# Sink tokens of a windowed attention in tiled matmuls: four column tiles for their scores, two row tiles for their AV, and a new order of the AV work

## The chip, the cores and the metric

The kernel runs on one core of a Trainium2 chip. A core has TensorE (PE: matmuls; its weight loads are listed apart as PEld), VectorE (DVE), ScalarE (ACT), GpSimd (POOL, which here also issues the input DMAs) and SyncE (SP, which issues DMAs). Matmuls write to PSUM, which the kernel uses as eight banks of 128 x 512 float32; VectorE and ScalarE read the results from there. The metric is the time of one execution in microseconds (us) on the device. Profiles come from one execution each, and their times are counted from the start of its span.

## The reference

Attention in which each query sees the first 4 keys (the sink) and the last 128, then a gated feed-forward network:

```python
batch, n_heads, seq, head_dim = (4, 8, 768, 64)      # n_sink 4, window 128
scores = scale * np.matmul(q, k.transpose(0, 1, 3, 2))
rel = pos[:, None] - pos[None, :]
keep = (pos[None, :] < n_sink) | ((rel >= 0) & (rel < window))
a = softmax(np.where(keep, scores, -1e9))             # over the keys
x = np.matmul(a, v)                                   # as (3072 tokens, 512)
xn = x / np.sqrt(np.mean(x * x, axis=-1, keepdims=True) + 1e-06) * rms_g
g = xn @ w_gate                                       # 512 -> 1536
out = (g * (1.0 / (1.0 + np.exp(-g))) * (xn @ w_val)) @ w_out
```

All inputs and the output are float32; the kernel works in bfloat16 with float32 sums.

## The kernel before

**Blocks and groups.** The 4 x 768 tokens are 24 blocks of 128 tokens: block g is tile t = g % 6 of batch b = g // 6. Four blocks make a group for the feed-forward network (FFN), so there are six groups.

**Attention of a block.** Queries and keys are transposed to `qkT` (features on partitions; two heads share 128 partitions) either on TensorE with a copy by ScalarE (`unit_t`, `unit_t1`) or, for later blocks, by DMA transposes that SP issues. `unit_s(g)` makes the scores of key block g against query blocks g and g + 1 in four PSUM banks (`pT`): eight matmuls over 64 partitions, two heads at a time in the upper and lower half of the array. ScalarE takes the exponential into `et`, and VectorE (batches 0 and 1) or GpSimd (2 and 3) masks it. `unit_av(g, u)` makes the attention output of four heads (half u) of query block g in one bank (`pv`): per head one matmul with the masked scores of key block g − 1 and one with those of block g, 65 columns each, of which the last is the sum of the weights. VectorE divides (`rden`, `x`), ScalarE squares and sums (`sq`, then a read of its accumulator), and after both halves VectorE makes the RMS factor (`m`, `y`) and the normalised rows `xr`. These are transposed to `xnt` on TensorE with a copy by ScalarE (`unit_x`, blocks 0 to 7) or by DMA through SP (from block 8).

**Sink keys.** Blocks with t of 0 and 1 have the sink inside their window; the other 16 blocks get it apart. `unit_sink(b)`, once per batch, makes two tiles. `ksk` holds the four sink keys of each pair of heads; its slices are placed so that a full 128-column weight puts head pair hp at 8 rows of the result from hp x 8 on. `vsk` holds the sink values of all heads on the rows of their own head, zero elsewhere: a matmul with `sel` repeats the values of the four sink tokens for every head (`pvs`), and VectorE multiplies by the mask `headm`. `unit_sink_scores(b, t)`, for t of 2 and 4, adds four full matmuls of 256 columns into one bank (`pss`, L321), which gives the sink scores of two query blocks, and ScalarE takes the exponential (`esk`). `unit_av` starts each half with one full 260-column matmul of `esk` with `vsk` (L444).

**FFN of a group.** For each of twelve feature tiles a gate part (`pg`: four matmuls, then tanh to `th` on ScalarE) and a value part (`pvl`: four matmuls, then two VectorE operations, `p` from `th` and `pg`, and `hT` from `p` and `pvl`). Then for each block of the group three output parts of four matmuls into one bank (`po`), a copy to `osb` by ScalarE and a DMA to the result. A part of the first group is smaller where a pair of feature tiles covers half the tokens.

**Order.** The order of PE and SP is written by hand; that of ScalarE, VectorE and GpSimd is made by a scheduler when the kernel is built and is then fixed. `step(g)` lists the attention work of one step in four slots, and `weave` lays the slots among the FFN parts, one about every 2.25 parts. In step g slot 0 holds the scores of block g (then, for some blocks, `unit_x(g - 3)`), slot 1 the first AV half of block g − 1 (and the sink units), slot 3 the second half, slot 1 or 2 the transposes of a later block. Before these steps stand a prologue and a first group whose order is written out. All PSUM tiles with tag `b1` come in turn from the same eight banks, so each new tile waits until the one eight tiles earlier has been read.

**GpSimd's queue.** It issues the loads of q, k, v and of the weights in a written order, with the selections that make `ident`, `amasks`, `sel` and `headm` among them.

Of the kernel before, what the change touches and what calls it, by code (L numbers as in the profile page):

```python
# [9 lines left out]
ALU = mybir.AluOpType  # L10
ACT = mybir.ActivationFunctionType
FP32 = mybir.dt.float32
BF16 = mybir.dt.bfloat16
I32 = mybir.dt.int32

P = 128
# [12 lines left out]
def kernel(  # L29
# [13 lines left out]
    nc = tc.nc  # L43

    B, H, S, D = q.shape
    DM = H * D
    DFF = moe_w_gate.shape[1]
    NS = int(n_sink)
    assert int(window) == P and NS == 4
    assert D == 64 and H == 8 and S % P == 0  # L50
    NT = S // P
# [4 lines left out]
    GB = 4  # L56
# [1 line left out]
    GN = GB * P  # L58
    VW = D + 1
    HW = 4 * VW  # L60
    KSW = P + 2 * NS
    inv_sqrt_d = 1.0 / math.sqrt(D)
    NEG = -32768.0
    RMS_EPS = 1e-6 * RSQRT_SCALE ** 2
# [86 lines left out]
    nc.vector.memset(amasks[:, 1, 0, :], 0.0)  # L151
    masks = const.tile([P, 2, 2, P], BF16, name="masks")

    sel = const.tile([P, P], BF16, name="sel")
    nc.vector.memset(sel, 0.0)
    headm = const.tile([P, H], BF16, name="headm")
    nc.vector.memset(headm, 1.0)

# [23 lines left out]
    with tc.manual_schedule(engines={mybir.EngineType.Pool, mybir.EngineType.DVE}):  # L184
        load_q(1)
        nc.gpsimd.affine_select(
            out=ident, in_=ident, compare_op=ALU.not_equal, fill=1.0,
            base=0, pattern=[[-1, P]], channel_multiplier=1,
        )
        nc.gpsimd.affine_select(  # L190
            out=amasks[:, 1, 0, :], in_=amasks[:, 1, 0, :], compare_op=ALU.is_ge,
            fill=NEG, base=0, pattern=[[1, P]], channel_multiplier=-1,
        )
        nc.vector.tensor_scalar(
            out=amasks[:, 1, 1, :], in0=amasks[:, 1, 0, :], scalar1=-1.0, scalar2=NEG,
            op0=ALU.mult, op1=ALU.add,
        )
        nc.vector.tensor_copy(out=amasks[:, 0, :, :], in_=amasks[:, 1, :, :])
        nc.vector.memset(amasks[0:NS, 0, :, :], 0.0)
        unit_cast(0)  # L200
        unit_cast(1)
        load_k(1)
        load_v(0)
        load_v(1)
        load_w(0)
        load_q(2)
        load_k(2)
        load_w(1)
        load_q(3)
        load_v(2)  # L210
        load_k(3)
        load_v(3)
        nc.gpsimd.affine_select(
            out=sel[:, 0:H * NS].rearrange("p (h s) -> p h s", s=NS),
            in_=sel[:, 0:H * NS].rearrange("p (h s) -> p h s", s=NS),
            compare_op=ALU.not_equal, fill=1.0,
            base=0, pattern=[[0, H], [-1, NS]], channel_multiplier=1,
        )
        nc.gpsimd.affine_select(
            out=headm, in_=headm, compare_op=ALU.is_ge, fill=0.0,  # L220
            base=0, pattern=[[-NS, H]], channel_multiplier=1,
        )
        nc.gpsimd.affine_select(
            out=headm, in_=headm, compare_op=ALU.is_ge, fill=0.0,
            base=NS - 1, pattern=[[NS, H]], channel_multiplier=-1,
        )
        load_w(2)
        load_w(3)
        load_q(4)
        load_w(4)  # L230
        load_k(4)
        load_w(5)
        load_v(4)
        for g in range(GB + 1, 2 * GB):
            load_q(g)
            load_k(g)
            load_v(g)
        load_wo(0)
        last_load = load_wo(1)
# [51 lines left out]
    def unit_sink(b):  # L291
        ks = sink.tile([P, HP * KSW], BF16, name="ksk")
        nc.vector.memset(ks, 0.0)
        ksv = ks.rearrange("p (h c) -> p h c", c=KSW)
        for hi in range(2):
            pr = slice(hi * D, (hi + 1) * D)
            nc.vector.tensor_copy(
                out=ksv[pr, :, hi * NS:(hi + 1) * NS],
                in_=QKT[b][pr, 1, :, 0:NS],
            )  # L300
        KSK[b] = ks
        vs = sink.tile([P, H, VW], BF16, name="vsk")
        for half in range(2):
            ps = pp[0].tile([P, 512], FP32, name="pvs", tag="b1")
            hs = slice(half * 4, half * 4 + 4)
            nc.tensor.matmul(
                out=ps[:, 0:HW], lhsT=sel, rhs=V16[b][:, 0, hs, :],
                start=True, stop=True,
            )
            nc.vector.tensor_tensor(  # L310
                out=vs[:, hs, :], in0=ps[:, 0:HW].rearrange("p (h c) -> p h c", c=VW),
                in1=headm[:, hs].unsqueeze(2).to_broadcast((P, 4, VW)), op=ALU.mult,
            )
        VSK[b] = vs

    def unit_sink_scores(b, t):

        w = 2 * P
        ps = pp[0].tile([P, 512], FP32, name="pss", tag="b1")
        for hp in range(HP):  # L320
            nc.tensor.matmul(  # L321
                out=ps[:, 0:w], lhsT=KSK[b][:, hp * P:(hp + 1) * P],
                rhs=QKT[b][:, 0, hp, t * P:(t + 2) * P],
                start=(hp == 0), stop=(hp == HP - 1),
            )
        es = sink.tile([P, w], BF16, name="esk", bufs=3)
        nc.scalar.activation(out=es, in_=ps[:, 0:w], func=ACT.Exp, scale=inv_sqrt_d)
        ESK[(b, t)] = es[:, 0:P]
        ESK[(b, t + 1)] = es[:, P:w]
# [105 lines left out]
    def halves(g):  # L435

        return [slice(0, DM // 2), slice(DM // 2, DM)] if g == 1 else [slice(0, DM)]

    def unit_av(g, u):
        b, t = divmod(g, NT)  # L440

        pv = pp[0].tile([P, 512], FP32, name="pv", tag="b1")
        if t >= 2:
            nc.tensor.matmul(  # L444
                out=pv[:, 0:HW], lhsT=ESK[(b, t)],
                rhs=VSK[b][:, 4 * u:4 * u + 4, :],
                start=True, stop=False, skip_group_check=True,
            )
        for i, h in enumerate(range(H)[heads_of(g, u)]):
            dest = pv[:, i * VW:(i + 1) * VW]  # L450
            if t >= 1:
# [184 lines left out]
    def step(g):  # L636
# [2 lines left out]
        b, t = divmod(g, NT)  # L639
        slots = [[], [], [], []]  # L640
        if g < NB:
            slots[0].append(lambda: unit_s(g))
            if t == 1:
                slots[1].append(lambda: unit_sink(b))
            if t in (2, 4):
                slots[1].append(lambda: unit_sink_scores(b, t))
        if g <= NB:
            slots[1].append(lambda: unit_av(g - 1, 0))
            slots[3].append(lambda: unit_av(g - 1, 1))
        if g - 3 < NB:  # L650
            slots[0].append(lambda: unit_x(g - 3))
        if g + 2 < NB and not by_dma(g + 2):
            slots[2 if t != 5 else 1].append(lambda: unit_t(g + 2))
        if g + 3 < NB and by_dma(g + 3):
# [59 lines left out]
    with tc.manual_schedule(engines=MANUAL):  # L714
# [6 lines left out]
        for ft in range(FA, FTN):  # L721
# [2 lines left out]
            [lambda: unit_t1(2, 1), lambda: unit_bias(1, 1), lambda: unit_sp(1, 1), lambda: unit_sink(0)],  # L724
            [lambda: unit_t1(3, 0), lambda: unit_s(2)],
            [lambda: unit_sink_scores(0, 2)],
            [lambda: unit_t1(3, 1), lambda: unit_bias(3, 0), lambda: unit_av(2, 0), lambda: unit_sp(3, 0), lambda: unit_av(2, 1)],
            [lambda: unit_av(3, 0)],
            [lambda: unit_av(3, 1), lambda: unit_t1(4, 0)],
            [lambda: unit_bias(3, 1), lambda: unit_sp(3, 1)],  # L730
            [lambda: unit_x(2)],
            [lambda: unit_t1(4, 1)],
            [lambda: unit_x(3)],
        ], first=True)
        slots = [[lambda: unit_t1(5, 0)], [lambda: unit_t1(5, 1)], [lambda: unit_s(4)], [lambda: unit_sink_scores(0, 4)], [lambda: unit_t(6)], []]
        for g in range(5, NB + 3):
            slots += step(g)
        slots[6].pop()
        slots[10].pop()
        outs = []  # L740
        n = 0
        for G in range(NG):
# [47 lines left out]
```

The softmax here doesn't subtract the row's maximum and nothing guards it: scores larger than these inputs give would overflow.

## Time and profile before

| | us |
|---|---|
| median of 4 runs (lowest to highest) | 254.87 (253.96 to 255.2) |
| the profiled execution's own time | 253.96 |
| its span, from the first to the last instruction | 252.2 |
| PE busy | 240.5 |
| VectorE busy | 180.5 |
| ScalarE busy | 139.4 |
| GpSimd busy | 97.8 |

The rows of the instructions that the diff touches (line, engine, operation, output from inputs, shapes, count, total busy us and mean ns of one; the array's rows and columns stand before the operand of a matmul):

```profile
L456 PE MATMUL pv<-v,et 128*128 128x65 bf16 x168 | 15.3, 193 | 0.0
L444 PE MATMUL pv<-vsk,esk 128*128 128x260 bf16 x32 | 8.8, 274 | 0.1
L321 PE MATMUL pss<-qkT,ksk 128*128 128x256 bf16 x32 | 4.8, 273 | 0.0
L327 ACT ACTIVATE esk<-pss 128x256 bf16<-128x256 f32 x8 | 3.3, 413 | 0.0
L310 DVE TENSOR_TENSOR vsk<-pvs,headm 128x260 bf16<-128x260 f32 x8 | 3.2, 419 | 0.0
L306 PE MATMUL pvs<-v,sel 128*128 128x260 bf16 x8 | 1.6, 277 | 0.0
L293 DVE MEMSET ksk<- 128x272 uint32 x4 | 1.1, 285 | 0.0
L219 POOL TENSOR_SCALAR_AFFINE_SELECT headm<-headm 128x8 bf16<-128x8 bf16 x1 | 0.3, 287 | 0.0
```

A matmul's duration runs to the modelled end of its pipeline, and the next one starts long before that, so the time that a matmul takes from PE is read from one start to the next and not from these means. In the answers in order of time the first number of a row is the start and the second the length in us; rows of equal instructions are merged (x8), and a bracket tells how long the engine was idle before and what ended it. A few matmul records are missing from the trace.

### The profile page before, as it was taken

The numbers are of one execution on the slowest core, as the hardware profiler recorded it, in microseconds if no ns is written. First come the engines' busy times: TensorE is split into PE (matmuls) and PEld (weight loads), VectorE is DVE, ScalarE is ACT, GpSimd is POOL, SyncE is SP. The second block draws the span as 40 slices with busy tenths as digits, with TensorE's granted clock in tenths as the row PEclk, the third lists the DMA queues.
The fourth block names the chain that finished last, engine by engine and source line by source line (L and its number), as shares of the span: only waits on it lengthen the run. The fifth ranks groups of instructions, "written<-read, shape, count | busy, mean of one in ns | idle before, by whom it ended". The sixth has DMA issues, their size and how long they took to land.

```text
span 252.2 us, 4804 instructions
## 1 busy us (share of the span) xinstructions
PE 240.5 (95%) x1733; PEld 128.5 (51%) x1760; DVE 180.5 (72%) x474; ACT 139.4 (55%) x312; POOL 97.8 (39%) x129
## 2 busy tenths in 40 slices
PE   6988989989999999999999999999999999999994
PEld 2537778755555454454454454454454544444441
DVE  5475898899778999439988459988359991287700
ACT  2567668789886465556474546466545341323211
POOL 8996778289986663134041004044301000000000
PEclk9999999999999999999999999999999999999999
DMA  9999999999999999950130550330321013200022
GB/s 130 151 173 192 187 157 189 184 155 150 194 185 166 150 129 154 165 141 8 21 60 6 146 146 3 64 61 17 112 84 23 0 21 100 89 0 0 0 86 83
DMA packets 105849, 25.74 MB, mean 102 GB/s; under 512 B 95073, under 2 KB 102753, under 8 KB 105826
## 3 DMA queue, kind: packets, MB, share of 16 engines
q0 software_dynamic: 80704, 13.90, 76.0%
q1 hardware_dynamic: 24082, 11.28, 19.0%
q10 hardware_dynamic: 1040, 0.26, 0.5%
q8 instruction: 14, 0.23, 0.4%
q14 instruction: 9, 0.07, 0.1%
HBM read 28.31 MB, written 6.29 MB: 137 GB/s over the span
## 4 chain that ended last, share of the span: by engine, by line
PE 72%; DMA 12%; POOL 7%; DVE 5%; issue 2%; ACT 1%; POOLq 0%; ACTq 0%; DVEq 0%
PE po L622 24%; PE pvl L581 19%; PE pg L581 19%; DMA ks<-in_k_dram 5%; DMA wv<-in_moe_w_val_dram 4%; DMA wg<-in_moe_w_gate_dram 3%; PE pT L413 3%; POOL v L124 2%; POOL qs L111 2%; PE pv L456 2%; PE pv L452 1%; PE pv L444 1%; DVE p L599 1%; POOL ks L111 1%; DVE hT L607 1%
## 5 line engine op out<-in xcount | busy, mean ns | idle before, releaser
L581 PE MATMUL pg<-xnt,wg 128*128 128x512 bf16 (+1 forms) x317 | 73.5, 352 | 1.4 <-ACT xnt L567 0.7
L581 PE MATMUL pvl<-xnt,wv 128*128 128x512 bf16 (+1 forms) x322 | 73.4, 353 | 0.3
L622 PE MATMUL po<-wo,hT 128*128 128x512 bf16 x279 | 64.9, 379 | 0.5 <-issue 0.2
L594 ACT ACTIVATE th<-pg 128x512 bf16<-128x512 f32 x72 | 42.9, 596 | 38.6 <-PE pg L581 38.5
L599 DVE SCALAR_TENSOR_TENSOR p<-th,pg 128x512 bf16<-128x512 bf16 x72 | 49.0, 680 | 20.2 <-ACT th L594 19.8
L607 DVE TENSOR_TENSOR hT<-p,pvl 128x512 bf16<-128x512 bf16 x72 | 49.3, 685 | 3.7 <-PE pg L581 0.5
L581 PEld LDWEIGHTS <-wg 128*128 128x128 bf16 x328 | 30.4, 98 | 27.3 <-issue 1.3
L581 PEld LDWEIGHTS <-wv 128*128 128x128 bf16 x328 | 30.5, 98 | 27.1 <-issue 1.1
L422 ACT ACTIVATE et<-pT 128x512 bf16<-128x512 f32 x76 | 39.8, 602 | 4.9 <-PE pT L413 4.7
L622 PEld LDWEIGHTS <-hT 128*128 128x128 bf16 x288 | 26.7, 98 | 29.7 <-issue 0.8
L390 POOL TENSOR_SCALAR_AFFINE_SELECT et<-et 128x512 bf16<-128x512 bf16 x20 | 13.1, 658 | 74.0 <-ACT et L422 74.0
L494 ACT ACTIVATE sq<-x 128x256 bf16<-128x256 bf16 x48 | 20.0, 417 | 26.5 <-DVE x L484 26.1
L629 ACT ACTIVATE osb<-po 128x512 f32<-128x512 f32 x24 | 14.4, 602 | 25.8 <-PE po L622 20.8
L111 POOL DMA_DIRECT2D qs<-in_q_dram x23 | 20.7, 898 | 9.1 <-DMA wo<-in_moe_w_out_dram 2.2
L111 POOL DMA_DIRECT2D ks<-in_k_dram x23 | 20.5, 893 | 5.7 <-DMA wo<-in_moe_w_out_dram 2.9
L124 POOL DMA_DIRECT2D v<-in_v_dram x24 | 21.4, 893 | 3.1 <-DMA wg<-in_moe_w_gate_dram 1.4
L484 DVE TENSOR_TENSOR x<-pv,rden 128x256 bf16<-128x256 f32 x48 | 20.2, 422 | 0.8
L541 DVE SCALAR_TENSOR_TENSOR xr<-x,y,gb 128x512 bf16<-128x512 bf16 (+1 forms) x25 | 19.9, 798 | 0.7
L479 DVE RECIPROCAL rden<-pv 128x4 f32<-128x4 f32 x48 | 8.4, 176 | 16.1 <-PE pv L456 15.9
L388 DVE TENSOR_TENSOR et<-et,masks 128x1024 bf16<-128x1024 bf16 (+1 forms) x22 | 13.9, 638 | 2.8 <-ACT et L422 2.7
L456 PE MATMUL pv<-v,et 128*128 128x65 bf16 x168 | 15.3, 193 | 0.0
L452 PE MATMUL pv<-v,et 128*128 128x65 bf16 x136 | 12.7, 193 | 0.0
(75 smaller groups left out, 216.1 us busy)
## 6 DMA issues: line engine op xcount, KB each, us to landing
out_dram<-osb SPq DMA_DIRECT2D x24, 256.0 KB, 2.1
v<-in_v_dram POOLq DMA_DIRECT2D x24, 128.0 KB, 7.5
qs<-in_q_dram POOLq DMA_DIRECT2D x23, 128.0 KB, 7.8
ks<-in_k_dram POOLq DMA_DIRECT2D x23, 128.0 KB, 7.8
wg<-in_moe_w_gate_dram POOLq DMA_DIRECT2D x6, 256.0 KB, 8.2
wv<-in_moe_w_val_dram POOLq DMA_DIRECT2D x6, 256.0 KB, 8.6
wo<-in_moe_w_out_dram POOLq DMA_DIRECT2D x2, 768.0 KB, 10.6
osb<-in_k_dram ACTq DMA_DIRECT2D x1, 256.0 KB, 4.6
```

Of the source, the lines that this page charges most:

```text
L111: nc.gpsimd.dma_start(out=tl, in_=src[b, :, t * P:(t + 1) * P, :].rearrange("h t d -> t h d"),)
L124: nc.gpsimd.dma_start(out=V16[b][:, t, :, 0:D], in_=v[b, :, t * P:(t + 1) * P, :].rearrange("h t d -> t h d"),)
L422: nc.scalar.activation(out=et[:, hi].rearrange("p j n c -> p (j n c)"), in_=banks[u][hi], func=ACT.Exp, scale=inv_sqrt_d,)
L456: nc.tensor.matmul(out=dest, lhsT=E[(g, h, 0)], rhs=V16[b][:, t, h, :], start=(t == 0), stop=True, skip_group_check=True,)
L484: nc.vector.tensor_tensor(out=X16[g][:, heads_of(g, u), :], in0=pvv[:, :, 0:D], in1=RDEN.pop((g, u)).unsqueeze(2).to_broadcast((P, 4, D)), ...
L494: nc.scalar.activation(out=sq, in_=xh, func=ACT.Square, scale=MS_SCALE, accum_out=MS[g][:, u:u + 1],)
L541: nc.vector.scalar_tensor_tensor(out=XR[g][-1], in0=x16[:, c], scalar=y[:, 4:5], in1=gb[:, c], op0=ALU.mult, op1=ALU.mult,)
L581: nc.tensor.matmul(out=ps[:, i * n:(i + 1) * n], lhsT=w_sb[:, kt, ft * P:(ft + 1) * P], rhs=XNT[G][:, kt, cols], start=(kt == 0), stop=(kt ...
L594: nc.scalar.activation(out=st["th"], in_=st["pg"], func=ACT.Tanh, scale=0.5)
L599: nc.vector.scalar_tensor_tensor(out=p1, in0=st["th"], scalar=1.0, in1=st["pg"], op0=ALU.add, op1=ALU.mult,)
L607: nc.vector.tensor_tensor(out=HT[key][:, i:i + n, cols], in0=p1.rearrange("p (n c) -> p n c", n=n), in1=pvl.rearrange("p (n c) -> p n c", ...
L622: nc.tensor.matmul(out=st["po"], lhsT=HT[(G, ft // 2)][:, ft % 2, tb * P:(tb + 1) * P], rhs=wo[:, ft, :], start=(ft == 0), stop=(ft == FTN ...
```

## The change

It does five things.

- Sink keys take 32 columns per pair of heads (`KSW = 32`), and `unit_sink_scores` writes four matmuls to four 32-partition strips of one bank, each started and stopped by itself, in place of four full matmuls that add up.
- `unit_sink` makes `vsk` with eight matmuls of 65 columns, one per head, each with another slice of a wider `sel` as its weight, so that the values land on the rows of their head; ScalarE copies the two banks. `headm` and its two GpSimd selections go.
- `unit_sink_av(g)`, new, allocates both AV banks of a block at once and writes the sink part of each from one half of the partitions (64 rows). `unit_av` goes on in these banks.
- In `step` all of the sink scores, scores, sink AV and both AV halves stand in slot 0, the sink scores first. `unit_x` moves from slot 0 to slot 1, and two calls that were taken out of the list by hand are now left out by its condition.
- In the first group, the order is written anew: the scores of block 3 now come ahead of the AV of block 2, and the sink scores ahead of the scores of block 4.

```diff
--- before.py
+++ after.py
@@ -58,7 +58,7 @@
     GN = GB * P
     VW = D + 1
     HW = 4 * VW
-    KSW = P + 2 * NS
+    KSW = 32
     inv_sqrt_d = 1.0 / math.sqrt(D)
     NEG = -32768.0
     RMS_EPS = 1e-6 * RSQRT_SCALE ** 2
@@ -151,10 +151,8 @@
     nc.vector.memset(amasks[:, 1, 0, :], 0.0)
     masks = const.tile([P, 2, 2, P], BF16, name="masks")
 
-    sel = const.tile([P, P], BF16, name="sel")
+    sel = const.tile([P, 2 * P], BF16, name="sel")
     nc.vector.memset(sel, 0.0)
-    headm = const.tile([P, H], BF16, name="headm")
-    nc.vector.memset(headm, 1.0)
 
 
 
@@ -211,18 +209,8 @@
         load_k(3)
         load_v(3)
         nc.gpsimd.affine_select(
-            out=sel[:, 0:H * NS].rearrange("p (h s) -> p h s", s=NS),
-            in_=sel[:, 0:H * NS].rearrange("p (h s) -> p h s", s=NS),
-            compare_op=ALU.not_equal, fill=1.0,
-            base=0, pattern=[[0, H], [-1, NS]], channel_multiplier=1,
-        )
-        nc.gpsimd.affine_select(
-            out=headm, in_=headm, compare_op=ALU.is_ge, fill=0.0,
-            base=0, pattern=[[-NS, H]], channel_multiplier=1,
-        )
-        nc.gpsimd.affine_select(
-            out=headm, in_=headm, compare_op=ALU.is_ge, fill=0.0,
-            base=NS - 1, pattern=[[NS, H]], channel_multiplier=-1,
+            out=sel[:, P:P + NS], in_=sel[:, P:P + NS], compare_op=ALU.not_equal,
+            fill=1.0, base=0, pattern=[[-1, NS]], channel_multiplier=1,
         )
         load_w(2)
         load_w(3)
@@ -303,13 +291,16 @@
         for half in range(2):
             ps = pp[0].tile([P, 512], FP32, name="pvs", tag="b1")
             hs = slice(half * 4, half * 4 + 4)
-            nc.tensor.matmul(
-                out=ps[:, 0:HW], lhsT=sel, rhs=V16[b][:, 0, hs, :],
-                start=True, stop=True,
-            )
-            nc.vector.tensor_tensor(
-                out=vs[:, hs, :], in0=ps[:, 0:HW].rearrange("p (h c) -> p h c", c=VW),
-                in1=headm[:, hs].unsqueeze(2).to_broadcast((P, 4, VW)), op=ALU.mult,
+            for i in range(4):
+                h = half * 4 + i
+                at = P - (32 * (h // 2) + NS * (h % 2))
+                nc.tensor.matmul(
+                    out=ps[:, i * VW:(i + 1) * VW], lhsT=sel[:, at:at + P],
+                    rhs=V16[b][:, 0, h, :], start=True, stop=True,
+                    skip_group_check=True,
+                )
+            nc.scalar.copy(
+                out=vs[:, hs, :], in_=ps[:, 0:HW].rearrange("p (h c) -> p h c", c=VW),
             )
         VSK[b] = vs
 
@@ -319,9 +310,10 @@
         ps = pp[0].tile([P, 512], FP32, name="pss", tag="b1")
         for hp in range(HP):
             nc.tensor.matmul(
-                out=ps[:, 0:w], lhsT=KSK[b][:, hp * P:(hp + 1) * P],
+                out=ps[32 * hp:32 * hp + KSW, 0:w],
+                lhsT=KSK[b][:, hp * KSW:(hp + 1) * KSW],
                 rhs=QKT[b][:, 0, hp, t * P:(t + 2) * P],
-                start=(hp == 0), stop=(hp == HP - 1),
+                start=True, stop=True,
             )
         es = sink.tile([P, w], BF16, name="esk", bufs=3)
         nc.scalar.activation(out=es, in_=ps[:, 0:w], func=ACT.Exp, scale=inv_sqrt_d)
@@ -436,16 +428,25 @@
 
         return [slice(0, DM // 2), slice(DM // 2, DM)] if g == 1 else [slice(0, DM)]
 
+    PVB = {}
+
+    def unit_sink_av(g):
+        b, t = divmod(g, NT)
+        for u in range(2):
+            PVB[(g, u)] = pp[0].tile([P, 512], FP32, name="pv", tag="b1")
+        for u in range(2):
+            pr = slice(u * D, (u + 1) * D)
+            nc.tensor.matmul(
+                out=PVB[(g, u)][:, 0:HW], lhsT=ESK[(b, t)][pr, :],
+                rhs=VSK[b][pr, 4 * u:4 * u + 4, :],
+                start=True, stop=False, skip_group_check=True,
+            )
+
     def unit_av(g, u):
         b, t = divmod(g, NT)
 
-        pv = pp[0].tile([P, 512], FP32, name="pv", tag="b1")
-        if t >= 2:
-            nc.tensor.matmul(
-                out=pv[:, 0:HW], lhsT=ESK[(b, t)],
-                rhs=VSK[b][:, 4 * u:4 * u + 4, :],
-                start=True, stop=False, skip_group_check=True,
-            )
+        pv = PVB.pop((g, u)) if t >= 2 else pp[0].tile(
+            [P, 512], FP32, name="pv", tag="b1")
         for i, h in enumerate(range(H)[heads_of(g, u)]):
             dest = pv[:, i * VW:(i + 1) * VW]
             if t >= 1:
@@ -639,16 +640,18 @@
         b, t = divmod(g, NT)
         slots = [[], [], [], []]
         if g < NB:
+            if t in (2, 4):
+                slots[0].append(lambda: unit_sink_scores(b, t))
             slots[0].append(lambda: unit_s(g))
             if t == 1:
                 slots[1].append(lambda: unit_sink(b))
-            if t in (2, 4):
-                slots[1].append(lambda: unit_sink_scores(b, t))
         if g <= NB:
-            slots[1].append(lambda: unit_av(g - 1, 0))
-            slots[3].append(lambda: unit_av(g - 1, 1))
-        if g - 3 < NB:
-            slots[0].append(lambda: unit_x(g - 3))
+            if (g - 1) % NT >= 2:
+                slots[0].append(lambda: unit_sink_av(g - 1))
+            slots[0].append(lambda: unit_av(g - 1, 0))
+            slots[0].append(lambda: unit_av(g - 1, 1))
+        if GB <= g - 3 < NB:
+            slots[1].append(lambda: unit_x(g - 3))
         if g + 2 < NB and not by_dma(g + 2):
             slots[2 if t != 5 else 1].append(lambda: unit_t(g + 2))
         if g + 3 < NB and by_dma(g + 3):
@@ -724,19 +727,17 @@
             [lambda: unit_t1(2, 1), lambda: unit_bias(1, 1), lambda: unit_sp(1, 1), lambda: unit_sink(0)],
             [lambda: unit_t1(3, 0), lambda: unit_s(2)],
             [lambda: unit_sink_scores(0, 2)],
-            [lambda: unit_t1(3, 1), lambda: unit_bias(3, 0), lambda: unit_av(2, 0), lambda: unit_sp(3, 0), lambda: unit_av(2, 1)],
-            [lambda: unit_av(3, 0)],
+            [lambda: unit_t1(3, 1), lambda: unit_bias(3, 0), lambda: unit_sp(3, 0), lambda: unit_sink_av(2), lambda: unit_av(2, 0), lambda: unit_av(2, 1)],
+            [lambda: unit_sink_av(3), lambda: unit_av(3, 0)],
             [lambda: unit_av(3, 1), lambda: unit_t1(4, 0)],
             [lambda: unit_bias(3, 1), lambda: unit_sp(3, 1)],
             [lambda: unit_x(2)],
             [lambda: unit_t1(4, 1)],
             [lambda: unit_x(3)],
         ], first=True)
-        slots = [[lambda: unit_t1(5, 0)], [lambda: unit_t1(5, 1)], [lambda: unit_s(4)], [lambda: unit_sink_scores(0, 4)], [lambda: unit_t(6)], []]
+        slots = [[lambda: unit_t1(5, 0)], [lambda: unit_t1(5, 1)], [lambda: unit_sink_scores(0, 4), lambda: unit_s(4)], [], [lambda: unit_t(6)], []]
         for g in range(5, NB + 3):
             slots += step(g)
-        slots[6].pop()
-        slots[10].pop()
         outs = []
         n = 0
         for G in range(NG):
```

## The prediction

> **What bounds the kernel now.** I read the page's busy shares and slices first, then the busy time by stretches, then who TensorE (PE) waited for, and last PE's instructions in order of time.
>
> ```profile
> span 252.2 us, 4804 instructions
> ...
> PE 240.5 (95%) x1733; PEld 128.5 (51%) x1760; DVE 180.5 (72%) x474; ACT 139.4 (55%) x312; POOL 97.8 (39%) x129
> ...
> PEclk9999999999999999999999999999999999999999
> ```
>
> ```profile
> 0.00:52.00 52.00, 45.70 (x461) 31.76 (x464) 37.32 (x116) 33.47 (x74) 39.67 (x55) 1.00 1.76 170
> ...
> 110.00:147.00 37.00, 36.74 (x257) 18.35 (x259) 29.04 (x72) 20.75 (x50) 6.91 (x10) 1.00 0.26 63
> ```
>
> The columns of the second fence are the stretch, its length, and the busy time of PE, weight loads, VectorE (DVE), ScalarE (ACT) and GpSimd. From 52 us on, PE streams without a hole at full clock (36.74 of 37 us). Before 52 us it has 6.3 us of holes. So after 52 us every streamed column that goes away counts in full; before it, what counts is what PE waits for.
>
> ```profile
> PE pxt L563 <- DVE xr L541: 1.3, 3, 0.7
> ...
> PE pg L581 <- ACT xnt L567: 0.7, 2, 0.5
> ...
> PE pqk L251 <- DMA ks<-in_k_dram: 0.6, 1, 0.6
> ```
>
> ```profile
> 50.40 0.40 PE L251 MATMUL pqk<-ident,qs 128*128 128x128 bf16 x4
> 51.37 0.40 PE L251 MATMUL pqk<-ident,ks 128*128 128x128 bf16 x4 [0.58 <-DMA ks<-in_k_dram]
> ```
>
> The third wait is the transposes of block 8: its q half runs at 50.40, its k half could follow 0.22 later but starts at 51.37, when the key block lands. Call it the block-8 wait: PE time won or lost before it counts only beyond its 0.74 us.
>
> ```profile
> 122.70 1.03 PE L581 MATMUL pvl<-xnt,wv 128*128 128x512 bf16 x4
> 123.56 1.03 PE L581 MATMUL pg<-xnt,wg 128*128 128x512 bf16 x4
> 124.52 0.61 PE L413 MATMUL pT<-qkT 64*128 64x256 bf16 x8
> 125.07 1.04 PE L581 MATMUL pvl<-xnt,wv 128*128 128x512 bf16 x4
> 125.94 1.03 PE L581 MATMUL pg<-xnt,wg 128*128 128x512 bf16 x3
> 126.80 0.60 PE L321 MATMUL pss<-qkT,ksk 128*128 128x256 bf16 x4
> 127.24 0.27 PE L444 MATMUL pv<-vsk,esk 128*128 128x260 bf16 x1
> 127.35 0.19 PE L452 MATMUL pv<-v,et 128*128 128x65 bf16 x1
> ```
>
> This gives the prices, start to start. A part of four 512-column matmuls is 0.86. One 256-column sink-score matmul is 0.11 (0.44 for four); one sink AV is 0.11; a 65-column AV is 0.03. The eight 64-row score matmuls take 0.55: as pairs side by side they would be four times 0.11, and the rest is two changes of tile shape. Entering costs 124.52 − 123.56 − 0.86 = 0.10, leaving about the same.
>
> **The change part by part** (us; minus is time saved; sums on the span).
>
> Sink scores. Eight units; two run before the block-8 wait. Each of the other six loses 4 × 0.11 and gets one pass of 0.11, if the four column tiles run side by side, plus one more change of shape, 0.10, since the row-tiled scores that follow would have changed it anyway: 6 × −0.22 = **−1.35**. No row has column tiles; the nearest are the 64-row pairs. From these: at best the switch is free (6 × −0.33 = −2.0); at worst the four run in turn (6 × +0.10 = +0.6). I take the pairs' behaviour.
>
> On this the Trainium skill speaks against the change. "TensorE: Matmul & The Clock Gate", Part 3, The mechanism, says that a weight load overlaps a matmul in flight only if its row group differs, and four column tiles share all row groups. Taken strictly, that is the case of tiles in turn, and this term would be +0.6. The same part also gives 2.38× for three column tiles, which would make it near −1.2, an estimate. No run here shows either yet.
>
> Sink AV. Twelve blocks after that wait have it; two matmuls of 0.11 become two 64-row ones side by side, in the shape that the scores before them have set: 12 × −0.11 = −1.3. Block 23 has no scores beside it and pays two changes, +0.2. Sum **−1.1** (−1.3 if that is free, +0.2 if the pair runs in turn).
>
> Sink values. Per batch two passes of 0.11 become eight of 0.03: 3 × 0.02, **+0.1** (eight more weight loads per batch; in AV the 0.03 already holds one each). VectorE loses eight products of 0.42; ScalarE gains eight copies, nearest row the 0.41 of the 128x256 sink exponential. ScalarE is not the bound, but at batch 0 its two copies stand ahead of a qkT copy that PE already waits for at 22.58 (0.67): +0.4 there, before the block-8 wait. Smaller memsets and two GpSimd selections fewer (0.29 and 0.19 at 14 us) lie under other work; at most the DMA issues behind them move up 0.4, and the landing with them.
>
> Order before the block-8 wait. The scores of block 3 now follow their own copy with no AV half (0.36) in between, and a lone sink AV pays two changes: +0.6. Against that go two score units and two sink AVs, about −0.6. A half AV of block 5 (52.47 to 52.92, 0.36) moves from behind the wait to before it; PE then arrives at about 51.1 instead of 50.6, still under the landing. So **−0.36**, and **+0.2** for arriving late (0 to +0.8).
>
> Transposes of x. They move one slot on. The one at 58.26 + 0.44 waits 0.35 for its xr today; with the AV ahead of it this goes: **−0.35**. The last one, of block 7, was ahead of eight output matmuls, the sink scores and a half AV (2.5 us) before the second group's first gate matmul (pg), which reads xnt. In the new order it stands directly before that gate matmul. On ScalarE its copy stands behind output, square and accumulator read, and the output waits for the matmuls just before the transposes:
>
> ```profile
> 70.08 0.41 ACT L494 ACTIVATE sq<-x 128x256 bf16<-128x256 bf16 x1
> 70.38 0.20 ACT L494 ACTIVATION_READ_ACCUMULATOR sq<-x 128x1 f32 x1
> 70.47 2.05 ACT L422 ACTIVATE et<-pT 128x512 bf16<-128x512 f32 x4
> 72.38 0.62 ACT L567 COPY xnt<-pxt 128x512 bf16<-128x512 bf16 x1
> 72.85 0.66 ACT L629 ACTIVATE osb<-po 128x512 f32<-128x512 f32 x1
> ```
>
> Output 0.5 (start to start), square with read 0.4, copy 0.6, about 0.2 from PE's last column to ScalarE's start, less the 0.22 that the transposes take: **+1.5** (+0.6 for the copy alone; +2.2 if the square waits for VectorE's x as well). Behind it stands all of PE.
>
> PSUM banks. Scores, both AV tiles, and in two steps the sink scores now take six or seven of eight banks within 1.3 us. The second AV tile and the next part need the banks of the last two or three parts. They get them in time if VectorE frees a value tile within 2.1 us of PE's end, or 1.45 us with sink scores. Today:
>
> ```profile
> 124.68 0.68 DVE L607 TENSOR_TENSOR hT<-p,pvl 128x512 bf16<-128x512 bf16 x1
> ...
> 157.47 0.67 DVE L607 TENSOR_TENSOR hT<-p,pvl 128x512 bf16<-128x512 bf16 x1
> ```
>
> The first is for the value part of 122.70 to 123.56, done 1.8 later; the second for one that ended at 154.85, done 3.3 later, the worst. Unhindered it is about 1.45. In the new order the AV work falls early in the step, so VectorE should be near 1.5 to 1.8 when the next burst comes: **+0.4** over seven steps (0 at 1.45; +9.7 if all were 3.3). A copy of qkT that now stands behind the sink-value copies of batch 1 may cost **+0.1**. On SP the DMA transpose of a finished xr now comes up ahead of the qkT transposes of a later block, which queue behind it; scores need those a step or more later, so the step's parts (nine of 0.86) cover it, as they do the masks and the earlier sink keys; bare, each would cost its own 0.4 to 1.4.
>
> Sum: −1.35 − 1.1 + 0.1 − 0.36 + 0.2 − 0.35 + 1.5 + 0.4 + 0.1 = **−0.9**. Span 252.2 becomes 251.3, the profiled time 253.96 (1.8 around the span) becomes 253.1. That execution was the fastest of four; against the median 254.87 it is 254.0.
>
> **The rivals.** Faster: VectorE's relief (8 × 0.42) clears the bank waits and the 0.2 wait at 161.5, PE is not late at the block-8 wait (0.2), which ends 0.4 earlier, and the copy before the gate matmul costs 1.0 instead of 1.5: 254.0 − 0.4 − 0.2 − 0.2 − 0.4 − 0.5 = 252.3, say 252.5. For it: the chain runs through VectorE from 153 to 162 us, where two of the products lie. Against: the output on ScalarE can't come sooner.
>
> Slower: the bank burst. If VectorE frees value tiles at 2.4 us when the burst comes, each of two steps with sink scores loses 0.95 and each of five others 0.3: 3.4 instead of 0.4, **257.0**. It decides from about 1.9 us on. For it: 2.8 and 3.3 us happen today. Against: they come when the late AV half lies just there.
>
> Column tiles in turn, so that the change doesn't do what it says: 254.0 + 6 × 0.33 = **256.0**. For it: nothing but the missing row; against: the 64-row pairs.
>
> **How the numbers follow.** Forecast 0.34, faster 0.32, banks 0.20, tiles in turn 0.14. A measurement here tells about 0.5% from no change (253.6 to 256.1). The forecast's own spread of ±1 gives a third to faster; the faster case counts four fifths as faster, the banks four fifths as slower, tiles in turn one half: faster 0.36, same 0.38, slower 0.26. Range 252.0 to 257.0; the forecast's own is 253.0 to 255.0.
>
> **What would show it.** Right: four pss matmuls in about 0.11 from first start to the scores less a 0.10 switch; the two sink AVs of a block starting together; k transposes of block 8 still waiting until near 51.3; a hole of about 1.5 us before the first gate matmul of the second group near 72 us, ended by ACT xnt; value tiles freed within 2 us at each burst. Wrong: pss starts 0.11 apart; holes of 0.3 or more before AV tiles; no hole near 72 us.

## The result, and the profile after

The changed kernel takes 255.58 us (median of 53 runs, 254.68 to 256.44) against 255.01 for the kernel before beside it (79 runs, 253.71 to 257.4). The ratio is 1.0027, with a 95% interval of 1.0018 to 1.0036: slower by 0.7 us (0.5 to 0.9), where 0.9 less was forecast. The profiled execution took 255.42, with a span of 253.7; the one before took 253.96 and 252.2.

First the page of the kernel after: its span, and its line of busy times.

```profile
span 253.7 us, 4856 instructions
...
PE 237.1 (93%) x1760; PEld 123.5 (49%) x1784; DVE 176.5 (70%) x465; ACT 141.9 (56%) x320; POOL 94.5 (37%) x127
```

PE is busy 3.4 us less than before and the span is 1.5 us longer: work did go away, and PE waits more than it saved. The list of what PE waited for in the kernel after tells where (us in total, times, longest):

```profile
PE pg L582 <- ACT xnt L568: 2.0, 2, 1.6
PE pqk L239 <- DMA qs<-in_q_dram: 1.3, 1, 1.3
PE pT L405 <- ACT qkT L274: 1.3, 2, 0.9
...
PE pv L439 <- DVE p L600: 0.7, 1, 0.7
PE pqk L239 <- DMA ks<-in_k_dram: 0.4, 1, 0.4
...
PE pv L439 <- DVE hT L608: 0.4, 1, 0.4
```

The wait of the transposes of block 8 for their keys (pqk behind the DMA of ks) is no longer in the list, and the wait of pxt for xr has shrunk (0.9 in all); the waits shown are new or longer. The two DMA waits, 1.3 and 0.4, are those of block 5, at 34 to 36 us.

PE in order of time at three places: the sink AVs of block 5 up to the scores of block 7, the second group's first gate matmul, and block 16 (start, length, line, operation; a bracket tells the idle time before a row):

```profile
47.84 0.27 PE L439 MATMUL pv<-vsk,esk 64*128 64x260 bf16 x1
48.83 0.27 PE L439 MATMUL pv<-vsk,esk 64*128 64x260 bf16 x1 [0.71 <-DVE p L600]
...
51.90 1.03 PE L582 MATMUL pvl<-xnt,wv 128*128 128x512 bf16 x4
53.80 0.61 PE L405 MATMUL pT<-qkT 64*128 64x256 bf16 x8 [0.88 <-ACT qkT L274]
...
73.56 0.39 PE L564 MATMUL pxt<-ident,xr 128*128 128x128 bf16 x4
75.52 0.81 PE L582 MATMUL pg<-xnt,wg 128*128 128x512 bf16 x3 [1.58 <-ACT xnt L568]
...
126.37 0.29 PE L312 MATMUL pss<-qkT,ksk 128*32 128x256 bf16 x4
126.59 0.61 PE L405 MATMUL pT<-qkT 64*128 64x256 bf16 x8
127.04 0.27 PE L439 MATMUL pv<-vsk,esk 64*128 64x260 bf16 x1
127.70 0.27 PE L439 MATMUL pv<-vsk,esk 64*128 64x260 bf16 x1 [0.39 <-DVE hT L608]
```

The scores of block 7 and the copy of block 8 in the kernel before, PE and then ScalarE:

```profile
52.47 0.27 PE L444 MATMUL pv<-vsk,esk 128*128 128x260 bf16 x1
...
52.92 0.61 PE L413 MATMUL pT<-qkT 64*128 64x256 bf16 x8
```

```profile
51.81 1.01 ACT L286 COPY qkT<-pqk 128x1024 bf16<-128x1024 bf16 x1 [0.54 <-PE pqk L251]
```

The gain: the four pss matmuls lie within 0.29 us, where one alone lasts 0.27 to 0.28; they run side by side. From the first of them to the first score is 0.22 us: 0.11 for the four, as for one matmul of 256 columns, and 0.11 left for the change of shape. Before, the four took 0.44. The two sink AVs of a block should start together, and at most blocks they do (block 23 among them).

The losses: the second sink AV waits for a bank that VectorE has not read yet, 0.99 for block 5 (48.83 against 47.84) and 0.66 for block 15, beside the scores of block 16. Two more waits for a bank, from start to start, are 0.24 for an output part at 100.11 (the AV matmul ahead of it starts at 99.84 and takes 0.03) and 0.30 for the second AV half of block 19 at 164.77. The scores of block 7 could start 0.96 after 51.90 (four matmuls 0.86, change of shape 0.10), and wait 0.94 more for ScalarE's copy of block 8. And the x transposes would be done 0.22 after 73.56, where the gate matmul starts at 75.52: 1.74 lost. ScalarE in order of time at the last two places tells why:

```profile
51.77 0.58 ACT L595 ACTIVATE th<-pg 128x512 bf16<-128x512 f32 x1
52.35 0.42 ACT L495 ACTIVATE sq<-x 128x256 bf16<-128x256 bf16 x1
...
52.76 0.99 ACT L274 COPY qkT<-pqk 128x1024 bf16<-128x1024 bf16 x1
...
73.98 0.58 ACT L630 ACTIVATE osb<-po 128x512 f32<-128x512 f32 x1
74.49 0.42 ACT L495 ACTIVATE sq<-x 128x256 bf16<-128x256 bf16 x1
...
74.91 0.56 ACT L568 COPY xnt<-pxt 128x512 bf16<-128x512 bf16 x1
```

Each copy that PE needs stands behind squares, the upper one behind a tanh and the lower one behind the output too. And no AV half lies between the transposes of block 8 and the scores of block 7 any more.

### The profile page after: what moved, and what is told of

It reads as the page before. It is cut to its first block, busy times and chain, and to the rows that moved or that the text cites. A ratio compares the mean times of both kernels' runs of the same rounds, so it can differ in the third digit from the quotient of the medians.

```text
span 253.7 us, 4856 instructions
## 1 busy us (share of the span) xinstructions
PE 237.1 (93%) x1760; PEld 123.5 (49%) x1784; DVE 176.5 (70%) x465; ACT 141.9 (56%) x320; POOL 94.5 (37%) x127
## 4 chain that ended last, share of the span: by engine, by line
PE 65%; DVE 11%; DMA 10%; ACT 7%; POOL 3%; issue 3%; POOLq 0%; DVEq 0%; ACTq 0%
PE po L623 20%; PE pvl L582 19%; PE pg L582 19%; DMA wv<-in_moe_w_val_dram 7%; DMA ks<-in_k_dram 3%; DVE hT L608 3%; DVE p L600 3%; PE pT L405 2%; DVE et L380 2%; ACT sq L495 2%; PE pv L453 2%; ACT et L414 2%; PE pv L457 1%; ACT qkT L274 1%; DVE x L485 1%
## 5 line engine op out<-in xcount | busy, mean ns | idle before, releaser
L623 PE MATMUL po<-wo,hT 128*128 128x512 bf16 x277 | 63.5, 379 | 0.7
L582 PEld LDWEIGHTS <-wg 128*128 128x128 bf16 x328 | 31.3, 98 | 30.4 <-issue 2.5
L582 PEld LDWEIGHTS <-wv 128*128 128x128 bf16 x328 | 31.1, 98 | 28.8 <-issue 0.2
L623 PEld LDWEIGHTS <-hT 128*128 128x128 bf16 x288 | 27.4, 98 | 30.6 <-issue 0.2
L542 DVE SCALAR_TENSOR_TENSOR xr<-x,y,gb 128x512 bf16<-128x512 bf16 (+1 forms) x25 | 18.1, 729 | 0.7
L480 DVE RECIPROCAL rden<-pv 128x4 f32<-128x4 f32 x48 | 7.8, 173 | 10.1 <-PE pv L457 10.0
L405 PE MATMUL pT<-qkT 64*128 64x256 bf16 (+1 forms) x168 | 12.0, 261 | 2.0 <-ACT qkT L274 1.3
L457 PE MATMUL pv<-v,et 128*128 128x65 bf16 x168 | 12.6, 194 | 0.0
```

Source lines behind the costliest of these rows:

```text
L542: nc.vector.scalar_tensor_tensor(out=XR[g][-1], in0=x16[:, c], scalar=y[:, 4:5], in1=gb[:, c], op0=ALU.mult, op1=ALU.mult,)
L582: nc.tensor.matmul(out=ps[:, i * n:(i + 1) * n], lhsT=w_sb[:, kt, ft * P:(ft + 1) * P], rhs=XNT[G][:, kt, cols], start=(kt == 0), stop=(kt ...
L623: nc.tensor.matmul(out=st["po"], lhsT=HT[(G, ft // 2)][:, ft % 2, tb * P:(tb + 1) * P], rhs=wo[:, ft, :], start=(ft == 0), stop=(ft == FTN ...
```

## The experiments

All times are medians; ratios are to the kernel before, run on the same chip beside each set (254.89 us with the first four, 254.94 with the others). Unless an edit says otherwise it is made to the changed kernel.

**Order and shapes apart.** The order of the changed kernel, with the tiles, sink values and sink AV matmuls of before (the inverse of the shape hunks):

```diff
-                out=ps[32 * hp:32 * hp + KSW, 0:w],
+                out=ps[:, 0:w], lhsT=KSK[b][:, hp * P:(hp + 1) * P],
...
-                out=PVB[(g, u)][:, 0:HW], lhsT=ESK[(b, t)][pr, :],
-                rhs=VSK[b][pr, 4 * u:4 * u + 4, :],
+                out=PVB[(g, u)][:, 0:HW], lhsT=ESK[(b, t)],
+                rhs=VSK[b][:, 4 * u:4 * u + 4, :],
```

> The changed kernel's order with the old tile shapes: full 128-row sink scores added up in one bank, full 128-row sink AV, sink values by VectorE with headm. Theory A (the shapes pay what the start-to-start times say, the order loses): slower than the changed kernel by 6 x 0.22 + 12 x 0.11 - 0.2, about 2.4, so 258.0, and 1.2% above the kernel before. Rival (the shapes pay little, the loss lies in them): at most 0.5 from the changed kernel, 255.1 to 256.1.

Measured: 257.92 us, ratio 1.0118 (1.0083 to 1.0152), as the first theory expected. The shapes are therefore worth (1.0118 − 1.0027) × 254.9 = 2.3 us, and the order costs 3.0. What PE waited for in this kernel is the same list, without a single tile of a new shape:

```profile
PE pg L589 <- ACT xnt L575: 1.7, 2, 1.5
PE pT L413 <- ACT qkT L286: 1.2, 2, 0.8
PE pv L446 <- DVE p L607: 0.5, 1, 0.5
```

So these three waits belong to the order: the hole before the second group's gate matmul, the copy of block 8 and the bank at block 5 (0.63 from start to start). The bank waits that come later belong to it only in part: behind blocks 12 and 15 PE waits 0.13 each in this kernel, where the changed kernel has 0.24 and 0.66, and at block 19 not at all, where it has 0.30. What is more there needs the shorter tiles as well as the order, so the 2.3 us of the shapes is what is left after it.

**The column strips alone.** The order of before, with column strips for the sink scores (ahead of the block's scores) and the sink values copied by ScalarE; the sink AV stays in full-height matmuls:

```diff
+            if t in (2, 4):
+                slots[0].append(lambda: unit_sink_scores(b, t))
             slots[0].append(lambda: unit_s(g))
             if t == 1:
                 slots[1].append(lambda: unit_sink(b))
-            if t in (2, 4):
-                slots[1].append(lambda: unit_sink_scores(b, t))
```

> The old order with the sink scores as four column strips (moved ahead of the scores of their step) and the sink values from TensorE by ScalarE; the sink AV stays two full matmuls within each half. Theory A: 6 x 0.22 = 1.3 under the kernel before, 253.7, since the AV halves and the transposes stay where they covered waits. Rival (ScalarE's eight extra copies and the sink scores ahead of the scores cost as much as the strips save): 255.0.

Measured: 254.42, ratio 0.9992 (0.9969 to 1.0015): 0.7 us more than expected, and not to be told from before. It lies between the two theories. The strips pay what they should in the later part: compared at the same feed-forward weight loads, PE stands 2.29 us behind the kernel before at 78 us and 1.35 at the end, 0.94 over four units, 0.23 each. What held it back lies earlier, and two long waits there are new, from its list:

```profile
PE pqk L239 <- DMA qs<-in_q_dram: 1.0, 1, 1.0
PE pss L312 <- ACT qkT L274: 0.7, 1, 0.7
```

The first is block 8, whose queries let PE on at 52.16 in this execution (50.40 before); the second is the copy of block 9, for which the sink scores at 60.73 wait. The profiled execution took 255.30, 0.9 above this kernel's median, and its waits at block 8 are about 1.0 longer than before (1.16 and 0.63 against 0.75). That fits a late landing in this execution alone, with the wait for the copy, 0.8 from start to start, as the miss of the median; one profile does not show it.

**The x transposes put back** at the end of a step's first slot:

```diff
         if GB <= g - 3 < NB:
-            slots[1].append(lambda: unit_x(g - 3))
+            slots[0].append(lambda: unit_x(g - 3))
```

> The changed kernel with one move undone: unit_x stands again in slot 0, at its end, so eight output matmuls lie between the transposes of block 7 and the first gate matmul that reads them. Theory A (the 1.75 us hole at 73.7 us is one term of the loss, and what follows is bound by PE): the hole shrinks to 0.3 or less and the time falls by 1.3 to 1.6, from 255.6 to about 254.2. Rival (the hole gives VectorE and ScalarE time that they need anyway, so it comes back as waits in the next stretch): less than 0.5 gained, 255.2 or more.

Measured: 254.19, ratio 0.9974 (0.9954 to 0.9993): 1.35 us less than the changed kernel ((1.0027 − 0.9974) × 254.9). The wait of pg for xnt in the second group is gone (the 0.2 in its list is the first group's, as before); the bank wait (1.14 at block 5) and the wait for the copy of block 8 (1.04) stay. The hole is a separate cost.

**The second AV half later**, in the third slot, behind the transposes, with the sink AVs left in the first:

```diff
             slots[0].append(lambda: unit_av(g - 1, 0))
-            slots[0].append(lambda: unit_av(g - 1, 1))
...
             slots[2].append(lambda: unit_t(g + 3))
+        if g <= NB:
+            slots[2].append(lambda: unit_av(g - 1, 1))
```

> The changed kernel with the second AV half moved from slot 0 to slot 2, behind the transposes there; both sink AVs stay beside the scores, so its bank is held longer. Theory B (the bank waits of 0.88, 0.65, 0.3 and 0.25 at 47.8, 127.0, 164.5 and 99.8 us come from both halves at once, and the 0.9 wait of the scores of block 7 from the missing AV half behind the transposes of block 8): these waits fall under 0.5 in sum, the wait for the key block 8 comes back with up to 0.7, and the time falls by 1.5 to 2, to about 253.8. Rival (a bank that is held over four parts makes the next burst wait): 256 or more.

Measured: 254.56, ratio 0.998 (0.9958 to 1.0003), 1.2 us less than the changed kernel and 0.8 more than expected. The bank wait of block 5 is gone and the scores of block 7 wait under 0.1 for their copy; one new bank wait, 0.5 for an output part, comes at 173 us. But PE now reaches the transposes of block 8 early, and the loads take part of it back (the keys let PE on at 52.30 in this execution, 51.37 before, so part of these waits is a later landing):

```profile
PE pqk L239 <- DMA qs<-in_q_dram: 0.9, 1, 0.9
PE pqk L239 <- DMA ks<-in_k_dram: 0.5, 1, 0.5
```

**Bank and copy apart.** The same, but into the second slot: out of the burst, yet still ahead of the transposes.

```diff
+            slots[1].append(lambda: unit_av(g - 1, 1))
```

> The changed kernel with only the second AV half moved to the second slot: one slot away from the burst, yet still ahead of the next transposes. It tells the two causes that e4 mended together apart. Theory A (banks and copy are separate: the burst fills the banks; the missing AV half behind the transposes uncovers the copy of block 8): bank waits shrink as in e4 to 0.6 us in all, the wait of 1.0 for the copy of block 8 before the scores of block 7 stays: 255.6 - 0.9 = 254.7 to 255.0. Rival B (the copy is late because the burst delays ScalarE): the wait for the copy goes too, 254.4 or below.

Measured: 254.97, ratio 1.0008 (0.9986 to 1.003), within what the first theory expected. The wait of 0.94 neither stayed nor went. PE, then ScalarE, then VectorE's two x of block 5, in this kernel:

```profile
51.90 1.03 PE L582 MATMUL pvl<-xnt,wv 128*128 128x512 bf16 x4
53.16 0.39 PE L405 MATMUL pT<-qkT 64*128 64x256 bf16 x4 [0.24 <-ACT qkT L274]
```

```profile
52.10 1.01 ACT L274 COPY qkT<-pqk 128x1024 bf16<-128x1024 bf16 x1 [0.46 <-PE pqk L239]
53.01 0.42 ACT L495 ACTIVATE sq<-x 128x256 bf16<-128x256 bf16 x1
```

```profile
51.87 0.42 DVE L485 TENSOR_TENSOR x<-pv,rden 128x256 bf16<-128x256 f32 x1
...
52.86 0.42 DVE L485 TENSOR_TENSOR x<-pv,rden 128x256 bf16<-128x256 f32 x1
```

PE passes the transposes of block 8 at the same time as in the changed kernel (both go on at 51.90). The copy now starts 0.66 earlier (52.10 against 52.76), because both squares of block 5 come behind it, and the scores wait 0.30 (51.90 + 0.96 = 52.86; they start at 53.16). So of the 0.94, about 0.3 is the missing AV half, and 0.64 is the squares ahead of the copy. ScalarE's order is fixed, and in the changed kernel the squares of block 5 come ahead of the copy: VectorE makes its two x at 50.89 and 51.83 there, and at 51.87 and 52.86 here. It is not shown whether, without the bank wait, those early squares would have been done before the copy was due. Both theories held in part. The bank waits did not fall to 0.6: the second sink AV of block 15 still waits (126.29 and 127.08, 0.79 apart), and value parts wait 0.34 at 48.81 and 0.27 at 90.39.

**Both mends together:**

> Both mends together: the x transposes back at the end of the step's first slot, and the second AV half in the third slot behind the transposes (the sink AVs stay first). Theory A (the changed order alone gave the gain of the tile shapes back, at three separate places: the second group's first gate matmul, the copy of block 8, the PSUM banks): the two mends add up, 255.6 - 1.4 - 1.0 = 253.1, no hole before the second group's first gate matmul, at most 0.2 us at the copy of block 8, bank waits of at most 0.3. Rival B (the places share one cover, or what one mend frees is lost at the next wait, such as the keys of block 8 landing at about 51): no better than the better of the two alone, 254.2. It beats the kernel before under A by 1.5 us or more.

Measured: 252.61, ratio 0.9921 (0.9899 to 0.9942): 2.0 us faster than before (1.5 to 2.6), and 2.7 faster than the changed kernel ((1.0027 − 0.9921) × 254.9). The mends of 1.35 and 1.2 add up. Its page, and what PE waited for from 38 us on:

```profile
span 250.5 us, 4874 instructions
...
PE 239.5 (96%) x1784; PEld 124.0 (49%) x1784; DVE 172.5 (69%) x465; ACT 142.2 (57%) x320; POOL 95.9 (38%) x127
```

```profile
PE pqk L239 <- DMA ks<-in_k_dram: 0.5, 1, 0.5
PE pss L312 <- ACT qkT L274: 0.4, 1, 0.4
...
PE pqk L239 <- DMA qs<-in_q_dram: 0.3, 1, 0.3
```

PE is busy for 96% of a span of 250.5. The x transposes of block 7 now have eight output matmuls behind them, and the gate matmul follows these at once (1.89 from start to start: eight of 0.216, and 0.16 of wait):

```profile
70.73 1.89 PE L623 MATMUL po<-wo,hT 128*128 128x512 bf16 x8
72.62 1.02 PE L582 MATMUL pg<-xnt,wg 128*128 128x512 bf16 x4
```

**The sink values on VectorE**, on top of both mends:

```diff
-            nc.scalar.copy(
+            nc.vector.tensor_copy(
                 out=vs[:, hs, :], in_=ps[:, 0:HW].rearrange("p (h c) -> p h c", c=VW),
```

> As e5_both, but the sink values are copied out of PSUM by VectorE (eight copies), not by ScalarE. Theory A' (the waits for qkT copies of block 9 and the like, 0.56 before the sink scores near 59 us in e4, come from the two sink-value copies of 0.4 each that stand ahead on ScalarE): those waits shrink by 0.4 or more in all, 252.7. Rival B' (the qkT copies are late for the exponentials ahead of them, and VectorE, with 0.4 per copy more, frees value tiles later): same as e5 within 0.3, or up to 0.5 slower.

Measured: 252.60, ratio 0.9911 (0.9895 to 0.9927), not to be told from the version without it; both theories allow this time. The wait of pss for the copy of block 9 does go, as the first theory says, but PE waits elsewhere: an AV at 59.63 us waits 0.24 (DVE hT 0.2 in the list), and po a little longer (0.4 for 0.3). Which engine copies the sink values makes no difference that this run can tell.


**The early order put back:** blocks 2 and 4 only.

```diff
-            [lambda: unit_t1(3, 1), lambda: unit_bias(3, 0), lambda: unit_sp(3, 0), lambda: unit_sink_av(2), lambda: unit_av(2, 0), lambda: unit_av(2, 1)],
+            [lambda: unit_t1(3, 1), lambda: unit_bias(3, 0), lambda: unit_sink_av(2), lambda: unit_av(2, 0), lambda: unit_sp(3, 0), lambda: unit_av(2, 1)],
...
-        slots = [[lambda: unit_t1(5, 0)], [lambda: unit_t1(5, 1)], [lambda: unit_sink_scores(0, 4), lambda: unit_s(4)], [], [lambda: unit_t(6)], []]
+        slots = [[lambda: unit_t1(5, 0)], [lambda: unit_t1(5, 1)], [lambda: unit_s(4)], [lambda: unit_sink_scores(0, 4)], [lambda: unit_t(6)], []]
```

> The changed kernel with the order of before in the two places ahead of the steps: the first AV half of block 2 ahead of the last scores of block 3, and the sink scores of block 4 in the slot behind the scores. Theory A (everything ahead of 36 us is absorbed by the wait for the keys of block 5, so that this part of the changed order neither costs nor gains): the time of the changed kernel within 0.3, 255.3 to 255.9, and TensorE reaches 38 us within 0.15 of the changed kernel. Rival B (the early order costs on its own): 0.5 or more faster than the changed kernel.

Measured: 255.40, ratio 1.0024 (1.0004 to 1.0044), the time of the changed kernel. The mark in the trace failed: PE reaches 38 us 0.9 earlier than in the changed kernel, mostly since it waited 0.8 and not 1.4 at the queries of block 5 (and 0.6 at its keys in both). The two profiled executions differ in when those loads let PE on. What they share is that PE was some 1.7 us ahead of before at 20 us and had lost 1.0 (this kernel) and 1.8 (the changed one) of that by 37 us. In the five other kernels with the early code of the changed kernel PE was within 0.4 of before at 20 us and did not wait for block 5, so that head start is no effect of the change.

## Why the prediction was wrong

It summed to −0.9 and the ratio says +0.7. The step that failed is the price of the new order: its terms (−0.36 + 0.2 − 0.35 + 1.5 + 0.4 + 0.1) came to +1.5, and the order alone measured +3.0 (2.1 to 3.9). By the experiments, in the prediction's own terms (us):

| term of the sum | forecast | measured, and how |
|---|---|---|
| sink scores, sink AV, sink values | −1.35 − 1.1 + 0.1 = −2.35 | −2.3 (±0.9), changed kernel against its order alone |
| the order as a whole: the two rows below | +1.49 | +3.0 (±0.9), order alone against before |
| transposes of x | −0.35 + 1.5 = +1.15 | +1.35 (±0.55), put back |
| second AV half early: half AV −0.36, late arrival +0.2, banks +0.4, copy +0.1 | +0.34 | +1.2 (±0.6) with the half in the third slot; +1.35 (±0.75) as the last step to both mends |

The shapes and the two parts of the order give −2.3 + 1.35 + 1.2 = +0.25, as near to +0.7 as their intervals allow to say. That the first row agrees to 0.05 is partly luck: it is known to ±0.9 only, and it is what is left after bank waits that the order alone does not have.

**Right:** the prices of the shapes. Column tiles behave as the 64-row pairs do, and so do the two sink AVs; a change of shape costs 0.10 to 0.11, entering or leaving. The rival of tiles in turn falls: pss to scores is 0.22 and not 0.54. The hole before the second group's gate matmul was named with its place, its cause and 1.5 us; it is 1.74, with two squares ahead of the copy where the prediction counted one.

**Wrong, first:** the step "A half AV of block 5 moves from behind the wait to before it ... So −0.36". What the half had been doing there was not asked. In the profile before, the copy of block 8 ran from 51.81 to 52.82 and the scores of block 7 began at 52.92, just behind it: the half AV at 52.47 was its cover. The step was booked as a gain although the prediction cites that very half with its times. Without it the scores wait, 0.94 in the profile after, of which the second-slot run shows 0.3 as the bare cover, which leaves almost nothing of the 0.36, and the rest as the squares ahead of the copy. A square ahead of the copy of block 10 gives 0.46 more (the scores at 65.09). The arrival at the block-8 wait was late indeed: the wait of 0.75 vanished, but mainly because PE had waited 0.99 for a bank before it.

**Wrong, second:** the size of "**+0.4** over seven steps" for the PSUM banks. In the profile after, the four waits are 0.99 (block 5), 0.24 (100.11 us), 0.66 (block 15) and 0.30 (164.77 us), 2.2 in all. The forecast had no wait if a value tile came free within 1.45 us with the sink scores in the burst, and took 1.5 to 1.8. For block 15 the value tile came free at 127.65, 2.2 after its matmuls (125.41). At block 5 it was not a value tile at all: the bank belonged to a gate tile, whose reader, VectorE's p, came behind the product for xr and behind a late tanh (VectorE, then ScalarE in order of time, kernel after):

```profile
47.42 0.75 DVE L542 SCALAR_TENSOR_TENSOR xr<-x,y,gb 128x512 bf16<-128x512 bf16 x1
48.09 0.68 DVE L600 SCALAR_TENSOR_TENSOR p<-th,pg 128x512 bf16<-128x512 bf16 x1
```

```profile
46.21 0.99 ACT L274 COPY qkT<-pqk 128x1024 bf16<-128x1024 bf16 x1
47.10 1.08 ACT L595 ACTIVATE th<-pg 128x512 bf16<-128x512 f32 x2
```

That p ends at 48.77, and the second sink AV starts at 48.83. The gate tile's matmuls ended at 45.56 (the next part starts there), but its tanh, the first of the two at 47.10, stood behind squares and a copy of qkT and ended at about 47.7. So p could not have begun before that: by these times the product for xr accounts for 0.4 of the 0.99 and the late tanh for the rest. The prediction looked at VectorE's value tiles alone. So the rival of the bank burst had the mechanism in part, and its 3.0 us more was too much: the waits came at four places, the first of them, at block 5, ahead of the block-8 wait. The prediction's own sign of being wrong, holes of 0.3 or more before AV tiles, was there.

These misses can be added up in the two profiled executions: banks 2.19 for 0.4, copies 0.94 + 0.46 + 0.06 for 0.1, the hole 0.24 more, and at block 8 a wait of 0.75 gone where 0.16 net had been booked, 1.79 + 1.36 + 0.24 − 0.59 = 2.8. The profiled times moved by 255.42 − 253.96 = +1.46 where −0.9 was forecast, 2.4 apart. Of the 0.4 between, 0.2 is a wait for p at 162 us of the kernel before, which is gone from the kernel after and stood only in the faster rival; the rest is not accounted for.

Two readings in the prediction are a little off. The "0.35" that the transposes at 59.06 waited for xr holds a change of shape of 0.10, so the wait is 0.26. And of the 0.55 of the eight score matmuls, the 0.11 beyond four passes is one change of shape, the one on leaving, since 0.55 is counted from their first start.

The Trainium skill bears on both sides of this. "TensorE: Matmul & The Clock Gate", Part 3, The mechanism, read strictly, would have had the four column tiles in turn; the trace shows four of them in 0.11 (0.22 to the next shape's first matmul) and decides. "TensorEngine Tiling (Array Packing)", Performance Considerations, PSUM Bottleneck, warns that tiling speeds up TensorE and not the emptying of PSUM, which may then become the limit. The 2.2 us of bank waits in the changed kernel agree with that in kind. But the run with the order alone waits 0.63 at block 5 too, and with both mends, the tiles unchanged, one bank wait of 0.5 is left (at 170.59): here it takes the order that brings the tiles together, and the shapes shorten the time between.

**What held of the block-8 wait:** in the third-slot run PE came to it early and waited there. Of block 5 the runs show less: with or without the early order the time is the same within the intervals.

## What to carry to other kernels

When work is moved off a place, ask first what it was hiding there: between a transpose and the matmuls that read its copy, a half AV of 0.36 us was worth 0.3, nearly its whole length. A cheaper instruction and the order that lets it be cheap are two changes; here the first was worth 2.3 us and the second cost 3.0, and as the dear parts of the order were not needed for the cheap tiles, putting two pieces of work back kept nearly the whole gain. A burst of PSUM tiles waits for whichever reader is late, the gate tile's as well as the value tile's; and AV work moved ahead on PE brought its ScalarE work ahead too, here two squares in front of a copy that PE needed (0.64).

## What was not expected of the hardware

Four 32-column tiles of 256 columns run side by side though they share all rows: 0.11 us for four, as for one. Going from column tiles straight to row tiles costs 0.11 us, about what it costs to go from the full array to either (0.10). At these three kinds of boundary, and back to the full array (0.09 to 0.10), a change of shape was paid once, about 0.1 us each time.
